# Two-level Strassen products in a gated FNet mix: the last couple of sequence product 3 at the second level, and four inner sums made by accumulating transfers

## The chip, the cores and the metric

The kernel runs on one core of one Trainium2 chip. The metric is the device time of one execution in microseconds; for the kernel before it is 1760.47 us, the median of three runs (1760.24 to 1760.79).

## The reference, cut to what matters

All matrices are float32: x is 2048 x 1024 (S x D), the sequence DFT 2048 x 2048, the hidden DFT 1024 x 1024, w1 1024 x 3584, w2 3584 x 1024.

```python
g = sigmoid((x * gate_w).sum(-1, keepdims=True))
a = einsum("bsd,ed->bse", x, dft_hid_re)
b = einsum("bsd,ed->bse", x, dft_hid_im)
y = einsum("ts,bse->bte", dft_seq_re, a) - einsum("ts,bse->bte", dft_seq_im, b)
h = einsum("bsd,df->bsf", x, w1) + b1
h = where(h > 0, h, 0) ** 2
out = g * y + (1 - g) * (einsum("bsf,fd->bsd", h, w2) + b2)
```

## The kernel before, in words

**Runs and products.** There are five large matrix products, which the code calls runs: x (both hidden DFTs), a and b (the two column parts of w1), c (the sequence DFT, its real and imaginary half stacked to 8 k-steps of 256 rows) and o (w2, 7 k-steps of 256). Each run is done with Strassen's scheme in Winograd's form: both matrices are cut in 2 x 2 quadrants, and seven products of sums of quadrants take the place of eight. `FACTORS` (line 40) names the left and the right factor of the seven: product 1 takes the quadrants (0, 0) and (0, 0), product 2 (0, 1) and (1, 0), product 3 the left sum S4 and the right quadrant (1, 1), product 4 (1, 1) and T4, and 5 to 7 take S1 and T1, S2 and T2, S3 and T3. "c3" is product 3 of the run c. `ORDER` (line 27) is the order in which TensorE takes the products of all runs: the three runs x, a, b first, then c1, c2, c5, c6, c3, c7, o1, c4, o2, o5, o6, o3, o7, o4.

**The second level.** Inside a product the scheme is used once more. In c and o (function `tall`, line 738) two k-steps that follow each other form a couple; the couple's 2 x 2 blocks are multiplied with seven inner products in place of eight. `TWICE_C` and `TWICE_O` (lines 37 and 38) say how many couples of a product are taken so; the k-steps that are left over are multiplied plainly, as `rest` (lines 767 and 869). Of the eight k-steps of a product of c, four couples use all and leave no `rest`; three couples leave two k-steps.

**Steps and matmuls.** A step is one left operand of 256 columns against one right operand of 512. A number in float32 is split in two float32r parts, `hi` (a conversion on ScalarE, line 238) and `lo` (the remainder, on VectorE, lines 244 and 246), and a step multiplies hi by hi, hi by lo and lo by hi. With two row blocks of 128 and two halves of the contraction that is 2 x 2 x 3 = 12 matmuls of 128x128 against 128x512 in c and o. A couple has seven steps; two plain k-steps have eight, for two left row halves against two right columns each.

**Sums.** The left sums of a couple are made in `Lefts` (line 463): S1 and S2 side by side in one tile, the difference S3 beside the first block, and S4, each by VectorE on 128x512, with 3.5 operands of 512 columns in all. The right ones are made in `Inner` (line 404) by `add` (line 214), one VectorE instruction of 128x1024 each. For couples whose first right block is kept in "turned" form, made ahead of time and stored, `TURN_R_SUMS` gives T2 as block (0, 1) plus block (0, 0), T1 as block (1, 1) less T2, and T4 as block (1, 0) less T2. A plain k-step whose block is stored turned needs one difference to turn it back (`plain_right`, line 829).

The sums of the outer level are made in `Side` (line 370). `BY_DMA` (line 63) names those that a transfer makes, for how many eighths of the positions: `accumulate` (line 203) loads one addend through SyncE's queue and lets GpSimd issue a transfer that adds the other from memory into the same tile. `THROUGH_C` (line 124) says for how many k-steps the outer sum T2 of c, made for c6 and used again in c4, is stored to memory and loaded again; for the others its tile is held from c6 to c4.

**Results of a product.** A product of c has four quarter results of two row blocks. Where another product's result has to be added (`old`), it is added by VectorE as soon as the first inner products are there, and the sum is reloaded into PSUM by ScalarE (`Group`, with `onto`) before the last inner products are summed onto it. With `late` (line 809, from `LATE`) the old result itself is reloaded, and what the product made is added at the end. A fourth group, for the plain k-steps alone, exists only where there is a `rest`.

**Order of the work.** TensorE's order is fixed. All other operations are entered in a list with the time at which they are needed: a step's operands by the step's place in TensorE's order, less a lead from `LEADS`, and everything before them backwards from there. A pass that is run when the program is built then gives each engine its own fixed order: at each moment it takes the first operation of the engine whose inputs are there, not more than `AHEAD` us before its due start, if one of the 55 tiles of 128x1024 float32 is free (`try_engine`, line 1566). `HALF` limits how many operands may have their `hi` without their `lo`. On the chip each engine then runs its order with semaphore waits only. `EARLY`, `TURNED_L` and `GATE` give dates to sums and differences that are made long before they are used. Loads go through SyncE's queue, stores and accumulating transfers through GpSimd's.

The matmuls are issued in line 1699; the sums of `add` are line 217, the left sums lines 481, 483, 488, 499 and 517, the additions from PSUM lines 356 and 358, the additions of two tiles line 366, the reloads of PSUM line 292.

Of the kernel before, what the change touches and what calls it, by code (L numbers as in the profile page):

```python
# [33 lines left out]
TWICE_X = (1, 2, 4, 5, 6, 7, 3)  # L34
TWICE_HA = (2, 3, 4, 5, 6, 7, 1)
TWICE_HB = (2, 4, 5, 6, 7, 1, 3)
TWICE_C = {1: 4, 2: 4, 3: 3, 4: 4, 6: 4, 5: 4, 7: 3}
TWICE_O = {1: 3, 2: 3, 3: 3, 4: 3, 6: 3, 7: 3, 5: 3}

FACTORS = {1: ((0, 0), (0, 0)), 2: ((0, 1), (1, 0)), 3: ("S4", (1, 1)), 4: ((1, 1), "T4"), 5: ("S1", "T1"),  # L40
# [19 lines left out]
MIX_R = {"T1": ((0, 0), (0, 1), ADD), "T2": ((1, 1), "T1", SUB), "T3": ((0, 1), (1, 1), SUB),  # L60
         "T4": ("T2", (1, 0), ADD)}
LESS_X, LESS_H, LESS_C, LESS_O = (3, 4), (3, 4, 5), (2, 6), (3, 4, 5)
BY_DMA = {'x_l': {'S1': 4, 'S2': 8, 'S3': 8, 'S4': 7}, 'x_r': {'T1': 5, 'T4': 8}, 'h_l': {'S4': 8, 'S3': 1}, 'c_l':
          {'S1': 7, 'S2': 7, 'S3': 8, 'S4': 8}, 'c_r': {'T1': 8, 'T2': 8, 'T3': 8, 'T4': 8}, 'o_l': {'S3': 8, 'S4':
          8}, 'o_r': {'T1': 8, 'T2': 8, 'T3': 8, 'T4': 8}}

AHEAD = {'SP': 13.4041, 'POOL': 13.1802, 'ACT': 13.8196, 'DVE': 10.3962}
FILL = {'DMA': 1.0243, 'ACT': 0.9397, 'DVE': 0.9869}
TAKE = 5.665
MARGIN = 0.79  # L70
NEAR = 0.0
URGENT = 1.997
KEEP = 5
EAGER = True
WARM = 38
LATE = {'c': (3,), 'o': (4, 5, 6, 7)}
DISTANT = (28.14, 4)
NARROW = (11.07, 3, 0.0)
LEADS = {208: 3.25, 209: 2.48, 210: 0.01, 212: 0.01, 213: -2.5, 186: 3.07, 216: 5.65, 199: 9.25, 200: 6.08, 201:
# [16 lines left out]
HURRY = 2.54  # L96
HALF = (2, 2.79)
BACKLOG = {"SP": 3.0, "POOL": 3.0}
PRELOAD = 30.0
EARLY_Q = (0, 1, 2, 3, 4, 5, 6, 7)  # L100
# [2 lines left out]
SUMMED = "xab"  # L103
ADD_S = ""
ADD_U = "bx"
EARLY = {'a_l': (('S2', 'S1'), (), 103.56, 2.103), 'b_l': (('S2',), (), 78.82, 4.245), 'x_r': (('T1',), (), 53.81,
         5.58)}
MERGE = 'sma'
STORES = "POOL"
# [2 lines left out]
REST = 0.886  # L112
GUARD = (0.874, 5.533)
SOON = {'POOL': 12.044, 'ACT': 5.5589, 'DVE': 6.9021}
SLACK = {'SP': 2.4281, 'POOL': 1.2495, 'ACT': 0.592, 'DVE': 0.4891}
LEAD = {'SP': 2.8064, 'POOL': 1.2123, 'ACT': 1.9836, 'DVE': 2.6943}
GATE = (268.4, 9.31)
WINDOW = 100
C_FORMS = ()
O_FORMS = ()  # L120
THROUGH_X = ("S1", "S2")
THROUGH_H = ("S2",)
THROUGH_W = ()
THROUGH_C = {'T2': 5}
THROUGH_O = {'T2': 8, 'S1': 2, 'S2': 2}
TURN_R = {'c': (0, 1, 2, 3), 'o': (0, 1, 2)}
TURN_L = {'c': (0, 1, 2), 'o': (0, 1)}
THIRD = {"c": (), "o": ()}
BACKWARD = {'c': (1, 4), 'o': (6,)}
TURNED_L = (((0, 0), (0, 1), (1, 0), (1, 1)), 100, 40)  # L130
TURNED_EARLY = (((0, 1), (1, 1), (0, 0), (1, 0)), 133, 30)
TURN_R_SUMS = {"T2": ((0, 1), (0, 0), ADD), "T1": ((1, 1), "T2", SUB), "T4": ((1, 0), "T2", SUB)}


@with_exitstack
def gated_mix_kernel(ctx: ExitStack, tc: tile.TileContext, x4, xn, w4, ct, w1a, w1b, w2, b1, b2, gw, out):
# [66 lines left out]
    def accumulate(v, src):  # L203
        w = Val("sum", v.width)
        Op("POOL", 0.6, 2 * P * 4 * v.width * 2, [v, src], w,
           lambda: nc.gpsimd.dma_start(w.ap(), src.at, accum_op=ADD), over=[v], must=True)
        return w
# [530 lines left out]
    def tall(name, left, right, ksteps, order, second, less, final, from_ps, by_row=None, turn=None, plain=None, turn_l=None,  # L738
# [5 lines left out]
        def product(p, old, quad):  # L744
# [45 lines left out]
            def inner(q):  # L790
                if q not in TURN_R[name]:
                    return Inner(lambda j, c: block(q, j, c), INNER_R)
                made = {}
                if turn and r in turn:
                    made[0, 1] = turn[r](q, block(q, 0, 1), block(q, 1, 1))
                inner_ = Inner(lambda j, c: block(q, j, c), TURN_R_SUMS)
                inner_.made.update(made)
                return inner_
# [1034 lines left out]
```

## Time and profile before

| | |
|---|---|
| median of three runs | 1760.47 us |
| the profiled execution, its own time | 1760.47 us |
| its span, first to last instruction | 1758.6 us |
| TensorE matmul, busy | 1752.1 us, 7748 instructions |
| VectorE, busy | 1700.1 us, 1659 instructions |
| ScalarE, busy | 1085.2 us, 1209 instructions |
| GpSimd, busy | 324.8 us, 468 instructions |
| mean busy share of the DMA engines, by slices of the span | 0.5 to 0.9 and more |
| bytes moved | 531.03 MB, 302 GB/s |
| granted clock of TensorE | 0.999 of full speed |

The 7748 matmuls are 38 small ones that warm the engine up and 7710 of the products. The profile's window view cuts the span into stretches and gives the busy time of each engine in each; its stretches are put at the borders of the products, which follow from the count of matmuls. A busy time there is the union of the engine's instructions, so that the overlap of one instruction's end with the next one's start is not counted twice. In the waits, a wait of a DMA queue (SPq) is one of the queue's own instructions, before it issues a transfer. In the names, PE is TensorE, DVE VectorE, ACT ScalarE, POOL GpSimd and SP SyncE. A tile that an operation overwrites in place keeps its old name, so an accumulating transfer can stand as `raw<-in_ct` on POOL's queue.

### The profile page before, as it was taken

To read this page: it belongs to the slowest core of one execution; us is meant where nothing else is said; L and a number is where in the kernel's file an instruction comes from. 1 tells how busy PE (TensorE), PEld (TensorE's weight loads), DVE (VectorE), ACT (ScalarE), POOL (GpSimd) and SP (SyncE) were. 2 spreads that over 40 slices of the span, in tenths; PEclk is the share of its full clock that TensorE was granted. 3 is DMA by queue.
4 is the path that set the end of the run, shared out by engine and by line. 5 is a ranking of instruction groups with operands and counts; after the bars stand their busy time and mean duration, and the time that the engine had idled before them with its cause. 6 is when DMAs were issued, how large, how long until landed. Compare 5 with 4: busy or idle time off the path is not lost.

```text
span 1758.6 us, 21932 instructions
## 1 busy us (share of the span) xinstructions
PE 1752.1 (100%) x7748; PEld 1451.3 (83%) x7748; DVE 1700.1 (97%) x1659; ACT 1085.2 (62%) x1209; POOL 324.8 (18%) x468
## 2 busy tenths in 40 slices
PE   9999999999999999999999999999999999999998
PEld 8888888888888888888888888888888888888887
DVE  8989999999999999899999999999999999999997
ACT  7445743334659674886747667475675676657754
POOL 0112212012211222101223121202101123212120
PEclk9999999999999999999999999999999999999999
DMA  9989999999999999889999999999859999999994
GB/s 354 413 324 349 358 375 380 397 342 362 328 346 352 337 290 329 305 304 272 281 259 191 278 294 296 271 337 274 233 164 335 330 262 290 308 282 296 277 224 79
DMA packets 156079, 531.03 MB, mean 302 GB/s; under 512 B 17057, under 2 KB 30721, under 8 KB 155969
## 3 DMA queue, kind: packets, MB, share of 16 engines
q0 software_dynamic: 65440, 233.88, 50.6%
q1 hardware_dynamic: 89824, 294.57, 44.9%
q8 instruction: 61, 1.00, 0.2%
q10 hardware_dynamic: 704, 1.18, 0.2%
q14 instruction: 50, 0.40, 0.1%
HBM read 401.10 MB, written 128.47 MB: 301 GB/s over the span
## 4 chain that ended last, share of the span: by engine, by line
PE 99%; DMA 0%; DVE 0%; ACT 0%; issue 0%
PE ps L1699 99%; DMA raw<-in_x 0%; ACT hi L1738 0%; DVE o L1212 0%; DVE o L1214 0%
## 5 line engine op out<-in xcount | busy, mean ns | idle before, releaser
L1699 PE MATMUL ps<-hi 128*128 128x512 f32 x2350 | 912.9, 389 | 0.6 <-ACT hi L1738 0.6
L1699 PE MATMUL ps<-lo,hi 128*128 128x512 f32 x2350 | 912.7, 389 | 0.0
L1699 PE MATMUL ps<-hi,lo 128*128 128x512 f32 x2350 | 912.7, 389 | 0.0
L1699 PEld LDWEIGHTS ps<-hi 128*128 128x128 f32 x2350 | 441.1, 188 | 92.2 <-ACT hi L1738 0.7
L1699 PEld LDWEIGHTS ps<-hi,lo 128*128 128x128 f32 x2350 | 441.2, 188 | 91.7
L1699 PEld LDWEIGHTS ps<-lo,hi 128*128 128x128 f32 x2350 | 441.2, 188 | 91.5
L238 ACT ACTIVATE hi<-raw 128x1024 fp32r<-128x1024 f32 (+1 forms) x402 | 406.3, 1040 | 169.5 <-PE ps L1699 91.4
L246 DVE TENSOR_TENSOR lo<-raw,hi 128x1024 fp32r<-128x1024 f32 (+1 forms) x348 | 411.4, 1204 | 2.8 <-DMA raw<-ab 1.3
L238 ACT ACTIVATE hi<-sum 128x1024 fp32r<-128x1024 f32 (+1 forms) x290 | 295.4, 1035 | 169.2 <-DVE sum L217 78.8
L246 DVE TENSOR_TENSOR lo<-sum,hi 128x1024 fp32r<-128x1024 f32 (+1 forms) x236 | 280.1, 1201 | 4.0 <-PE ps L1699 1.9
L345 ACT ACTIVATE acc<-ps 128x1024 f32<-128x1024 f32 (+1 forms) x153 | 150.9, 991 | 158.7 <-PE ps L1699 142.3
L358 DVE TENSOR_TENSOR acc<-acc,ps 128x1024 f32<-128x1024 f32 (+1 forms) x142 | 159.0, 1127 | 19.9 <-PE ps L1699 19.3
L1699 PE MATMUL ps<-hi,both 128*128 128x512 f32 x440 | 144.1, 389 | 0.0
L217 DVE TENSOR_TENSOR raw<-raw 128x1024 f32<-128x1024 f32 (+1 forms) x114 | 130.4, 1160 | 0.0
L292 ACT ACTIVATE ps<-acc 128x1024 f32<-128x1024 f32 (+1 forms) x79 | 77.2, 981 | 83.8 <-DVE acc L358 49.7
L1699 PEld LDWEIGHTS ps<-hi,both 128*128 128x128 f32 x440 | 82.6, 188 | 17.1
L217 DVE TENSOR_TENSOR sum<-raw,sum 128x1024 f32<-128x1024 f32 (+1 forms) x81 | 96.3, 1189 | 0.4 <-PE ps L1699 0.3
L1699 PE MATMUL ps<-lo,both 128*128 128x512 f32 x220 | 85.6, 389 | 0.0
L366 DVE TENSOR_TENSOR acc<-acc 128x1024 f32<-128x1024 f32 x69 | 83.0, 1215 | 1.2 <-ACT acc L345 1.2
L358 DVE TENSOR_TENSOR back<-back,ps 128x1024 f32<-128x1024 f32 x64 | 71.2, 1122 | 1.9 <-PE ps L1699 1.2
L217 DVE TENSOR_TENSOR sum<-raw 128x1024 f32<-128x1024 f32 (+1 forms) x57 | 68.1, 1197 | 2.0 <-DMA ab<-back 1.9
L244 DVE SCALAR_TENSOR_TENSOR lo<-raw,hi 128x1024 fp32r<-128x1024 f32 (+1 forms) x54 | 63.3, 1176 | 4.7 <-ACT hi L238 4.0
(96 smaller groups left out, 1051.3 us busy)
## 6 DMA issues: line engine op xcount, KB each, us to landing
raw<-in_ct SPq DMA_DIRECT2D x104, 512.0 KB, 7.4
raw<-h SPq DMA_DIRECT2D x79, 512.0 KB, 9.6
raw<-in_w SPq DMA_DIRECT2D x75, 512.0 KB, 9.1
back<-v SPq DMA_DIRECT2D x54, 512.0 KB, 8.1
raw<-ab SPq DMA_DIRECT2D x42, 512.0 KB, 7.1
raw<-h POOLq DMA_DIRECT2D x42, 512.0 KB, 11.6
raw<-in_ct POOLq DMA_DIRECT2D x41, 512.0 KB, 11.7
sum<-t SPq DMA_DIRECT2D x36, 512.0 KB, 8.5
```

Source lines behind the costliest of these rows:

```text
L217: Op("DVE", c, l, [a, b], w, lambda: nc.vector.tensor_tensor(w.ap(), a.ap(), b.ap(), op=op), over=[a, b])
L238: nc.scalar.activation(self.hi()[:, k, :], src(v)[:, k, :], AF.Copy, scale=-1.0 if less else 1.0)
L244: nc.vector.scalar_tensor_tensor(a, b, -1.0, c, op0=ALU.mult, op1=SUB)
L246: nc.vector.tensor_tensor(a, b, c, op=SUB)
L292: lambda rp=rp, k=k, e=e, v=v: nc.scalar.activation(self.ps[rp][:, :k, :], v.tile[:, e:e + k, :], AF.Copy),
L345: group.take(seg, rp, Op("ACT", c, l, [], w, lambda: nc.scalar.activation(view(w.tile, rows, rp), view(group.ps[rp], rows, rp), AF.Copy, s ...
L358: nc.vector.tensor_tensor(a, b, d, op=ADD)
L366: Op("DVE", c, l, [a, b], w, lambda: nc.vector.tensor_tensor(view(w.tile, rows, rp), view(a.tile, rows, rp), view(b.tile, rows, rp), op=op ...
L1699: nc.tensor.matmul(group.ps[r // group.per][:, r % group.per, :], a()[:, kk, r * P:(r + 1) * P], b()[:, kk, :], start=first and kk + n == ...
```

## The change

1. `TWICE_C[3]` goes from 3 to 4: the k-steps 6 and 7 of c3 become a fourth couple.
2. A new table `T2_DMA` and two lines in `inner`: for product 1 of c and product 2 of o, the inner right sum T2 of the couples 0 and 1 is made by an accumulating transfer. It loads block (0, 1) into a tile of its own and adds block (0, 0) from memory. The blocks themselves are still loaded as operands.
3. `THROUGH_C` goes from 5 to 8: the outer sum T2 of c is stored and loaded again for all eight k-steps.
4. `BY_DMA`: of the sums T4 of the x run three of four positions are made by transfers, where it was all four; of the sums S3 of w1's left side one position of four, where it was none (1 and 3 eighths of four positions make none and one), in each of a and b.
5. `LATE` takes in the products 1 and 2 of c beside 3. Product 1 has no old result, so only c2 is different.
6. Numbers of the pass that orders the work: leads, limits and dates.

```diff
-TWICE_C = {1: 4, 2: 4, 3: 3, 4: 4, 6: 4, 5: 4, 7: 3}
+TWICE_C = {1: 4, 2: 4, 3: 4, 4: 4, 6: 4, 5: 4, 7: 3}
...
-BY_DMA = {'x_l': {'S1': 4, 'S2': 8, 'S3': 8, 'S4': 7}, 'x_r': {'T1': 5, 'T4': 8}, 'h_l': {'S4': 8, 'S3': 1}, 'c_l':
+BY_DMA = {'x_l': {'S1': 4, 'S2': 8, 'S3': 8, 'S4': 7}, 'x_r': {'T1': 5, 'T4': 7}, 'h_l': {'S4': 8, 'S3': 3}, 'c_l':
...
-AHEAD = {'SP': 13.4041, 'POOL': 13.1802, 'ACT': 13.8196, 'DVE': 10.3962}
+AHEAD = {'SP': 12.9725, 'POOL': 13.1802, 'ACT': 13.8196, 'DVE': 10.3962}
...
-URGENT = 1.997
+URGENT = 1.945
...
-LATE = {'c': (3,), 'o': (4, 5, 6, 7)}
+LATE = {'c': (1, 2, 3), 'o': (4, 5, 6, 7)}
...
-LEADS = {208: 3.25, 209: 2.48, 210: 0.01, 212: 0.01, 213: -2.5, 186: 3.07, 216: 5.65, 199: 9.25, 200: 6.08, 201:
+LEADS = {208: 3.25, 209: 2.48, 210: 0.01, 212: -2.5, 213: -2.5, 186: 3.07, 216: 5.65, 199: 9.25, 200: 6.08, 201:
...
-HALF = (2, 2.79)
+HALF = (3, 2.85)
...
-EARLY = {'a_l': (('S2', 'S1'), (), 103.56, 2.103), 'b_l': (('S2',), (), 78.82, 4.245), 'x_r': (('T1',), (), 53.81,
+EARLY = {'a_l': (('S2', 'S1'), (), 103.56, 2.103), 'b_l': (('S2',), (), 93.23, 3.09), 'x_r': (('T1',), (), 53.81,
...
-SLACK = {'SP': 2.4281, 'POOL': 1.2495, 'ACT': 0.592, 'DVE': 0.4891}
-LEAD = {'SP': 2.8064, 'POOL': 1.2123, 'ACT': 1.9836, 'DVE': 2.6943}
-GATE = (268.4, 9.31)
+SLACK = {'SP': 2.4281, 'POOL': 1.2741, 'ACT': 0.592, 'DVE': 0.4891}
+LEAD = {'SP': 2.8064, 'POOL': 0.954, 'ACT': 1.9836, 'DVE': 2.6943}
+GATE = (244.0, 12.76)
...
-THROUGH_C = {'T2': 5}
+THROUGH_C = {'T2': 8}
...
-TURNED_L = (((0, 0), (0, 1), (1, 0), (1, 1)), 100, 40)
+TURNED_L = (((0, 0), (0, 1), (1, 0), (1, 1)), 64.3, 44.13)
...
+T2_DMA = {'c': {1: 2}, 'o': {2: 2}}
...
                 made = {}
+                if q < T2_DMA[name].get(p, 0) and isinstance(r, tuple):
+                    made["T2"] = accumulate(right[2 * q, 1].of(r), right[2 * q, 0].get(*r))
                 if turn and r in turn:
```

Of `LEADS`, a table from a step's number to us, about half of the entries differ and some hundred are new; one line of it stands here.

## Rows read from the trace of the kernel before

**Rows 1.** Waits of TensorE: line, waited for: us in total, times, longest.

```profile
PE warm L1748 <- DVE ones L1745: 1.1, 1, 1.1
PE ps L1699 <- ACT hi L1738: 0.6, 1, 0.6
```

**Rows 2.** The chain that ended last, in order of time: start us, us, what.

```profile
0.74 3.96 DMA raw<-in_x
...
5.71 1748.03 PE ps L1699 x7710
```

**Rows 3.** Windows: length, busy us (instructions) PE, PEld, DVE, ACT, POOL; clock, DMA share, GB/s.

```profile
738.90:815.10 76.20, 76.20 (x338) 63.12 (x337) 76.20 (x78) 57.36 (x64) 5.14 (x10) 1.00 0.85 301
815.10:891.30 76.20, 76.20 (x337) 62.95 (x336) 74.43 (x72) 51.61 (x54) 16.48 (x20) 1.00 0.97 265
...
967.50:1043.60 76.10, 76.10 (x337) 63.06 (x336) 75.22 (x76) 49.23 (x53) 13.08 (x18) 1.00 0.98 292
1043.60:1122.50 78.90, 78.90 (x349) 65.35 (x349) 74.23 (x72) 48.39 (x51) 16.47 (x21) 1.00 1.03 287
1122.50:1201.40 78.90, 78.90 (x349) 65.34 (x348) 78.39 (x77) 45.92 (x48) 9.80 (x14) 1.00 0.93 294
1201.40:1269.50 68.10, 68.10 (x302) 56.41 (x301) 68.10 (x68) 46.39 (x49) 13.29 (x16) 1.00 0.99 279
1269.50:1345.60 76.10, 76.10 (x338) 63.02 (x337) 73.61 (x72) 50.24 (x53) 3.36 (x5) 1.00 0.65 234
1345.60:1413.70 68.10, 68.10 (x302) 56.43 (x301) 68.10 (x65) 43.42 (x48) 12.04 (x15) 1.00 0.99 298
...
5.70:738.90 733.20, 733.19 (x3235) 607.28 (x3236) 701.66 (x685) 418.69 (x494) 138.64 (x229) 1.00 0.99 351
738.90:1685.70 946.80, 946.80 (x4178) 784.08 (x4177) 936.33 (x915) 623.37 (x665) 176.58 (x226) 1.00 0.97 278
```

**Rows 4.** Waits of VectorE from 738.9 to 1685.7 us: total, times, longest.

```profile
DVE acc L358 <- PE ps L1699: 2.8, 1, 2.8
DVE lo L246 <- PE ps L1699: 2.6, 5, 1.3
DVE lo L246 <- DMA raw<-ab: 1.3, 1, 1.3
```

**Rows 5.** Waits of SyncE's DMA queue from 738.9 to 1753 us.

```profile
SPq L200 <- PE ps L1699: 428.3, 138, 13.6
```

**Rows 6.** Timeline of VectorE at the end of c3: start us, us, instruction.

```profile
1092.22 4.62 DVE L246 TENSOR_TENSOR lo<-raw,hi 128x1024 fp32r<-128x1024 f32 x4
1096.76 1.21 DVE L217 TENSOR_TENSOR sum<-raw 128x1024 f32<-128x1024 f32 x1
1097.90 0.68 DVE L481 TENSOR_TENSOR sum<-raw 128x512 f32<-128x512 f32 x1
1098.50 3.48 DVE L246 TENSOR_TENSOR lo<-raw,hi 128x1024 fp32r<-128x1024 f32 x3
...
1105.38 4.61 DVE L246 TENSOR_TENSOR lo<-raw,hi 128x1024 fp32r<-128x1024 f32 x4
...
1114.57 1.22 DVE L358 TENSOR_TENSOR acc<-acc,ps 128x1024 f32<-128x1024 f32 x1 [2.83 <-PE ps L1699]
```

**Rows 7.** DMA issues: queue, count, KB each, median us to landing.

```profile
raw<-in_ct SPq DMA_DIRECT2D x104, 512.0 KB, 7.4
raw<-h SPq DMA_DIRECT2D x79, 512.0 KB, 9.6
...
raw<-h POOLq DMA_DIRECT2D x42, 512.0 KB, 11.6
raw<-in_ct POOLq DMA_DIRECT2D x41, 512.0 KB, 11.7
sum<-t SPq DMA_DIRECT2D x36, 512.0 KB, 8.5
...
raw<-turned SPq DMA_DIRECT2D x20, 512.0 KB, 6.3
```

38 rows, old and new, of the table LEADS are left out of this document.

## The prediction

> **What bounds the kernel now.** I read the waits of TensorE first: after its 38 warm-up matmuls it waits once, 0.6 us, for the first operand [rows 1]. Then the chain that ended last: 3.96 us of the first load, its conversion, and from 5.71 us on 7710 matmuls in 1748.03 us without a hole [rows 2]. That is 1748.03 / 7710 = 0.22672 us a matmul. So the time is the number of matmuls times 0.22672, with 5.71 us ahead of it and 4.9 us behind it in the span of 1758.6. The profiled execution took 1760.47 us, which is also the median of the three runs; the 1.9 us beside the span stay.
>
> The matmuls cut the span into products: the x, a and b products take 3234 matmuls, so c1 begins at 5.71 + 3234 x 0.22672 = 738.9; a product of c with four couples takes 28 x 12 = 336, one with three 348, one of o 300. In the windows by product, TensorE is busy for the whole of each, at a granted clock of 1.00, the level of 2.4 GHz [rows 3]. The second column to read is VectorE's: 76.20 of 76.20 in c1, 68.10 of 68.10 in o1 and o2. From c1 to the end of o7 it is busy 936.33 of 946.80 us, so it idles 10.47 us; in c3 it idles 4.67, in c4 2.49, in c2 1.77 [rows 3]. Its waits in that stretch are for a matmul to end or a transfer to land, few and short [rows 4]. Loads are not late either: SyncE's queue itself waited 428.3 us in 138 waits for TensorE to give a tile free [rows 5]. TensorE is the wall, VectorE stands just behind it, and tiles limit how far ahead the rest can work.
>
> **The change, part by part.** *The fourth couple of c3.* Two k-steps taken plainly cost 2 x 4 steps = 96 matmuls; as a couple they cost 7 steps = 84. Twelve fewer, 7698 in all: 12 x 0.22672 = 2.72 us off TensorE. No other part touches the count of matmuls.
>
> VectorE pays for it. Its pace is read from starts, since one instruction's end overlaps the next: four of 128x1024 start at 1092.22 and the next at 1096.76, so 4.54 / 4 = 1.135 us each; one of 128x512 at 1097.90 is followed at 1098.50, so 0.60 [rows 6]. Plainly the two k-steps need 2 left and 4 right low parts and one right difference: 7 wide instructions. As a couple they need 7 right and 3 left wide low parts, the right sums T2, T1, T4 (13 wide), and on the left one narrow low part and four narrow sums (5 narrow). 13 x 1.135 + 5 x 0.60 - 7 x 1.135 = +9.81 us. Quarter results cost the same: one addition from PSUM becomes one from tiles. ScalarE gets 4.5 more conversions and loses one reload of PSUM, some 4 us; it is busy 48.39 of 78.90 in c3 [rows 3], so nothing. The number of loads doesn't change: five right tiles either way.
>
> *T2 by transfer.* Four wide sums leave VectorE, two in c1 and two in o2: 4 x 1.135 = 4.54 us less. Each becomes one more load on SyncE's queue and an accumulating transfer on GpSimd's. Accumulates of this kind, with tiles as destination, land in 11.7 us (from the matrix, c1) or 11.6 us (from h, o2), after a load of 6.3 or 9.6 us [rows 7]. Through VectorE the chain is a load of 7.4 and 1.135 us. Started at the same moment, the new chain for c1 is 6.3 + 11.7 - 7.4 - 1.1 = 9.5 us later. I take nothing for it on TensorE: the schedule issues loads ahead of need, and 83 accumulates of these two kinds are already there [rows 7] without one wait of TensorE [rows 1]. The cover is the tile held about 10 us longer; if it is gone, T1, which subtracts T2, is late, then its two parts, then a step. Bounds: 0, and 9.5 us for each of four couples, 38 us. In GpSimd's queue the accumulate waits for its load; behind it stand the stores of c1's quarters, read much later, and o2's other accumulates, operands of o5. GpSimd is busy 5.14 us of c1 and 12.04 of o2 [rows 3], so little queues there.
>
> First the row: a plain load of the matrix by SyncE lands in 7.4 us, the accumulate by GpSimd in 11.7 [rows 7]. The Trainium skill says in "DMA: Bandwidth & Descriptors" (SWDGE vs HWDGE vs iDMA) that only GpSimd can issue accumulating transfers, and in "SBUF — State Buffer" (Who interferes with whom) that a VectorE instruction with two SBUF inputs contends with GpSimd's reads, and that a transfer held up by VectorE is one GpSimd makes. By that rule moving a sum off a full VectorE puts it on the one queue that a full VectorE can hold up, and the sum would be that of the late accumulates below; the longer landing agrees in sign, but the row can't say how much of it is the addition itself.
>
> *T2 of the outer sums through memory for k-steps 5 to 7.* Six stores more in c6 and six loads more in c4; six tiles are no longer held across c3, c7 and o1. c4's transfers are busy 0.65 of the time, c6's 0.98 [rows 3]. At nothing: o1's 68 us cover the loads for c4's first couple. Above: one load late, 8.5 us [rows 7]. Below: the free tiles let VectorE work further ahead, which can remove idle time there but no matmul.
>
> *The rest.* Of the left sums S3 one position of four goes to transfers in a and in b, and one T4 of the x stage comes back to VectorE: about one addition fewer before c1, where VectorE idles 31 us of 733 [rows 3]. c2's old quarters join at the end instead of midway: ten VectorE instructions and three reloads both ways. The new leads, dates and limits only reorder. All nothing, between -0.3 and +0.3 us, since TensorE's start hangs on the first load alone [rows 2] and nothing but a wait can add.
>
> **The sum** against the profiled execution: 1760.47 - 2.72 = 1757.75, if TensorE still never waits. Whether it does is VectorE's balance. From c1 to o7: 936.33 + 9.81 - 4.54 = 941.60 us of work in 946.80 - 2.72 = 944.08, so 2.48 us of idle time may stay of 10.47. In c3 alone, 74.23 + 9.81 = 84.04 us of work meet 78.90 - 2.72 = 76.18: 7.86 too much. Working ahead in c1's freed 2.27 us leaves 5.6 us by which VectorE comes closer to TensorE than before. How far ahead was it there? At 1105.38 it already made the first four low parts of c7, whose matmuls begin at 1122.5, 17 us later, and then sat idle 2.83 us for a matmul to end [rows 6]. Five and a half of these 17 us can go. After that c7's and c4's idle time (0.51 + 2.49) and o2's 2.27 give 5.3 back. So the likeliest is no wait: 1757.8.
>
> **Rivals.** *Some of the lead is missing where it is needed.* VectorE comes 5.6 us closer at c7's start, a few operands come late, and TensorE waits 0.6 to 6 us in all: 1758.4 to 1764. For it: VectorE is at 100% in c1, o1 and o2. Against: its lead of 17 us. Chance 0.20, more of it at the low end.
>
> *VectorE becomes the bound (the other side).* Its idle time is not lead to spend but made of waits that come again: for matmuls to end (2.8 and 2.6 us) and for transfers (1.3 us) [rows 4]. If all 10.47 us stay, TensorE must give 10.47 - 2.48 = 8.0 us, and the time is 1765.8. It decides slower once more than 6.24 + 2.48 = 8.7 us of the 10.47 stay, since 2.72 + 3.52 us must be lost (0.2% is 3.52 us, about what a measurement of this kernel can tell from no change). Against: in c3 half of the idle time is 2.83 us at its end with c7's work already made. Chance 0.08.
>
> *Late accumulates.* One couple late by the whole 9.5 us gives 1767.3, all four 1795.8. Against: the 83 that are on time. Chance 0.03.
>
> *It doesn't do it.* If the fourth couple were not taken, the count stayed 7710 and the time 1760.5; the code leaves no such way. Chance 0.01.
>
> *Faster by over 0.2%.* 3.52 us need another 0.8 us from the start or the end, which hang on the first load and the last two additions; 0.03.
>
> **How the numbers follow.** The forecast, no wait beyond 0.6 us, has 0.65. Within 0.2%: 0.65 + 0.20 + 0.01 = 0.86; slower 0.08 + 0.03 = 0.11; faster 0.03. The range begins at 1757.2 (a start half a microsecond sooner) and reaches to 1761.5, which takes in about three quarters of the waiting case, 0.15: 0.80 in all.
>
> **What would show it.** Right: 7698 matmuls after the warm-up in about 1745.3 us, no wait of TensorE longer than 0.6 us, c3's window at 76.2 us with VectorE full and its 2.83 us wait gone; VectorE's busy time about 4.4 us up (9.81 - 4.54 - 0.9); 42 loads of stored sums into a sum's tile where there were 36 [rows 7]; 20 transfers of 512 KB more in all. Wrong: TensorE waiting for a low part or its sum near 1120 to 1200, or for T1 in the second half of c1 or the first of o2 with an accumulate as its cause; or VectorE idle by 10 us again while TensorE waits.

## The result, and the profile after

The changed kernel takes **1763.66 us** (median of 15 runs, 1762.94 to 1765.52) against 1760.50 for the kernel before beside it (15 runs): ratio 1.0016, 95% interval 1.0009 to 1.0023. It is slower by 3.2 us, which is within 0.2%. The profiled execution took 1763.37 us with a span of 1761.5. The forecast was 1757.8, the range ended at 1761.5.

The page of the kernel after: busy time of each engine with its share of the span and its instructions, then the two lines of the chain that ended last.

```profile
PE 1751.3 (99%) x7736; PEld 1448.0 (82%) x7736; DVE 1704.6 (97%) x1665; ACT 1089.3 (62%) x1213; POOL 332.6 (19%) x479
...
PE 95%; DVE 3%; DMA 1%; issue 1%; POOL 0%; ACT 0%; DVEq 0%
PE ps L1710 95%; DVE lo L255 1%; DMA t<-raw 1%; DVE lo L253 0%; DVE sum L226 0%; DVE back L375 0%; DMA raw<-in_x 0%; DVE acc L375 0%; DVE sum L526 0%; DVE o L1223 0%; DVE o L1225 0%; DVE sum L492 0%; DVE raw L226 0%; DVE both L253 0%; ACT h
```

TensorE issued 7736 matmuls where it had 7748: the twelve are gone. VectorE is 4.5 us busier than before. But the chain, which was TensorE alone from 5.71 us on [rows 2], now leaves it for VectorE, 3% of the span. The waits of TensorE (line, waited for: us in total, times, longest; the lines of the code behind the edit in `inner` stand 11 lower than before, so 1710 is 1699 of [rows 1]; those between the tables and that edit stand 9 lower, so 255 is 246 and 226 is 217):

```profile
PE ps L1710 <- DVE lo L255: 3.7, 4, 1.5
...
PE ps L1710 <- ACT hi L1749: 0.5, 1, 0.5
```

Four waits for low parts are new. The view counts only a gap behind a matmul's modelled end; counted by starts, that is as the distance from one matmul's start to the next, it is more. The first matmul starts at 5.45 us and the last at 1756.28, and 7697 steps of 0.22672 us are 1745.06, so 1756.28 - 5.45 - 1745.06 = **5.8 us** is waiting. The account closes: -2.72 for the matmuls, -0.26 for the earlier start, +5.8 for the waits are +2.8 of the 2.9 us between the two profiled executions. So the saving came in full, and twice as much was lost to waits. Where, the windows by product show (length, busy us of PE, PEld, DVE, ACT, POOL with their instructions; clock, DMA share, GB/s), in the order c1, c2, c5, c6, c3, c7, o1, as [rows 3] has them but for c5:

```profile
738.60:814.80 76.20, 76.20 (x338) 62.89 (x337) 76.20 (x77) 58.27 (x66) 7.99 (x13) 1.00 0.91 319
814.80:891.00 76.20, 76.20 (x338) 63.10 (x337) 71.74 (x69) 48.77 (x51) 13.71 (x17) 1.00 0.92 263
891.00:968.60 77.60, 76.44 (x338) 62.98 (x337) 74.95 (x75) 51.57 (x56) 26.12 (x33) 1.00 1.04 230
968.60:1046.50 77.90, 76.42 (x337) 62.73 (x336) 77.75 (x80) 53.02 (x56) 16.60 (x24) 1.00 1.01 311
1046.50:1124.40 77.90, 76.81 (x338) 63.07 (x337) 77.90 (x76) 47.92 (x50) 14.44 (x18) 1.00 0.98 279
1124.40:1203.40 79.00, 78.97 (x349) 65.06 (x348) 79.00 (x78) 46.66 (x49) 9.96 (x13) 1.00 1.04 337
1203.40:1271.80 68.40, 68.36 (x301) 56.13 (x301) 68.40 (x67) 45.67 (x48) 12.87 (x16) 1.00 0.99 284
```

c5, c6 and c3 should last 336 x 0.22672 = 76.2 us and last 77.6, 77.9 and 77.9. In c6, c3, c7 and o1 VectorE is busy 303.05 of 303.20 us: it has nothing left. In c6 alone it runs 80 instructions where it ran 76 [rows 3], in c3 76 for 72. Yet just ahead of that stretch it sits idle: 4.46 us in c2 and 2.65 in c5, together 7.1, where it was 1.77 [rows 3] and 0.11, by the window of c5 before:

```profile
891.30:967.50 76.20, 76.20 (x338) 63.09 (x337) 76.09 (x77) 49.53 (x53) 24.63 (x31) 1.00 1.01 220
```

What it waited for there (from 738.6 to 968.6 us):

```profile
DVE lo L255 <- PE ps L1710: 3.5, 5, 1.3
DVE sum L526 <- PE ps L1710: 2.0, 1, 2.0
DVE lo L253 <- ACT hi L247: 0.7, 1, 0.7
DVE sum L436 <- PE ps L1710: 0.4, 1, 0.4
...
```

Nearly 6 of the 7 us are waits for a matmul to end. A low part and a sum read nothing that TensorE makes, so what a matmul's end gives them must be the tile to write to, which TensorE has then read for the last time; this is inferred from who ended the wait. The first wait of TensorE, at 914.45 us, is such a case itself. The chain around it, start us, us, what:

```profile
899.91 13.16 PE ps L1710 x58
...
913.17 1.24 DVE lo L255
...
914.45 5.74 PE ps L1710 x24
```

A matmul ends, that lets one low part start, and the next matmul waits 1.4 us for this part. The second and third wait, 1.6 us at 1014.30 and 1.5 from 1050.44 on by starts, are of the other kind. The second, in the timeline of TensorE and of VectorE (start us, us, instruction, idle time before it and who ended that); from 984 to 1053 us VectorE has no idle time:

```profile
1012.43 0.39 PE L1710 MATMUL ps<-hi 128*128 128x512 f32 x1
1014.30 0.50 PE L1710 MATMUL ps<-lo,hi 128*128 128x512 f32 x1 [1.48 <-DVE lo L255]
```

```profile
1012.41 0.69 DVE L526 TENSOR_TENSOR sum<-raw,sum 128x512 f32<-128x512 f32 x1
1013.02 2.36 DVE L255 TENSOR_TENSOR lo<-raw,hi 128x1024 fp32r<-128x1024 f32 x2
```

The third:

```profile
1049.60 0.39 PE L1710 MATMUL ps<-hi 128*128 128x512 f32 x1
1050.44 0.50 PE L1710 MATMUL ps<-lo,hi 128*128 128x512 f32 x1 [0.45 <-DVE lo L255]
1051.58 0.50 PE L1710 MATMUL ps<-hi,lo 128*128 128x512 f32 x1 [0.63 <-DVE lo L255]
```

```profile
1040.60 4.64 DVE L255 TENSOR_TENSOR lo<-raw,hi 128x1024 fp32r<-128x1024 f32 x4
1045.14 1.24 DVE L226 TENSOR_TENSOR raw<-raw,sum 128x1024 f32<-128x1024 f32 x1
1046.28 2.38 DVE L255 TENSOR_TENSOR lo<-sum,hi 128x1024 fp32r<-128x1024 f32 x2
1048.55 0.71 DVE L492 TENSOR_TENSOR sum<-sum,raw 128x512 f32<-128x512 f32 x1
1049.15 3.51 DVE L255 TENSOR_TENSOR lo<-raw,hi 128x1024 fp32r<-128x1024 f32 x3
```

Two low parts in a row come late, by 0.61 and 0.91 us, while VectorE goes from one instruction to the next without a gap. Here its order holds more work than there is time. The store in the page's chain (`DMA t<-raw`, 17.65 us up to 1040.23) kept nothing waiting: the low part behind it starts at 1040.60, 1.14 us after VectorE's instruction ahead of it, which is VectorE's own pace.

### The profile page after: what moved, and what is told of

Its sections match the earlier page's. It is cut to its first block, busy times and chain, and to the rows that moved or that the text cites. A ratio compares the mean times of both kernels' runs of the same rounds, so it can differ in the third digit from the quotient of the medians.

```text
span 1761.5 us, 21886 instructions
## 1 busy us (share of the span) xinstructions
PE 1751.3 (99%) x7736; PEld 1448.0 (82%) x7736; DVE 1704.6 (97%) x1665; ACT 1089.3 (62%) x1213; POOL 332.6 (19%) x479
## 2 busy tenths in 40 slices
DMA packets 158958, 541.52 MB, mean 307 GB/s; under 512 B 17376, under 2 KB 31040, under 8 KB 158848
## 4 chain that ended last, share of the span: by engine, by line
PE 95%; DVE 3%; DMA 1%; issue 1%; POOL 0%; ACT 0%; DVEq 0%
PE ps L1710 95%; DVE lo L255 1%; DMA t<-raw 1%; DVE lo L253 0%; DVE sum L226 0%; DVE back L375 0%; DMA raw<-in_x 0%; DVE acc L375 0%; DVE sum L526 0%; DVE o L1223 0%; DVE o L1225 0%; DVE sum L492 0%; DVE raw L226 0%; DVE both L253 0%; ACT hi L1749 0%
## 5 line engine op out<-in xcount | busy, mean ns | idle before, releaser
L255 DVE TENSOR_TENSOR lo<-raw,hi 128x1024 fp32r<-128x1024 f32 (+1 forms) x349 | 421.1, 1235 | 3.7 <-PE ps L1710 1.8
L247 ACT ACTIVATE hi<-sum 128x1024 fp32r<-128x1024 f32 (+1 forms) x294 | 299.8, 1037 | 164.1 <-DVE sum L226 92.5
L255 DVE TENSOR_TENSOR lo<-sum,hi 128x1024 fp32r<-128x1024 f32 (+1 forms) x239 | 288.5, 1225 | 4.7 <-PE ps L1710 2.4
L367 DVE TENSOR_TENSOR acc<-acc,ps 128x1024 f32<-128x1024 f32 (+1 forms) x144 | 162.7, 1137 | 14.8 <-PE ps L1710 12.1
L226 DVE TENSOR_TENSOR raw<-raw 128x1024 f32<-128x1024 f32 (+1 forms) x116 | 134.5, 1178 | 0.0
L226 DVE TENSOR_TENSOR sum<-raw,sum 128x1024 f32<-128x1024 f32 (+1 forms) x77 | 92.7, 1208 | 0.7 <-PE ps L1710 0.5
L215 POOL DMA_DIRECT2D raw<-h x44 | 41.1, 1069 | 135.2 <-DMA raw<-h 56.2
## 6 DMA issues: line engine op xcount, KB each, us to landing
raw<-h POOLq DMA_DIRECT2D x44, 512.0 KB, 11.7
t<-raw POOLq DMA_DIRECT2D x40, 512.0 KB, 14.4
```

Of the source, the lines that this page charges most:

```text
L226: Op("DVE", c, l, [a, b], w, lambda: nc.vector.tensor_tensor(w.ap(), a.ap(), b.ap(), op=op), over=[a, b])
L247: nc.scalar.activation(self.hi()[:, k, :], src(v)[:, k, :], AF.Copy, scale=-1.0 if less else 1.0)
L255: nc.vector.tensor_tensor(a, b, c, op=SUB)
L367: nc.vector.tensor_tensor(a, b, d, op=ADD)
```

## The experiments

Three theories stand. **Work** (A): with the couple, VectorE has more to do between c5 and o1 than that stretch holds, and TensorE waits for what is left over. **Order and tiles** (B): the work would fit, but low parts stand too far back in VectorE's fixed order or find no tile. **The side effects**: the accumulating transfers come late (C), or c2's late join moves additions into the full stretch (D). A further question came up with the first answers (E in the expectations): is the time that VectorE has ahead of the full stretch of any use in it? There A1 is theory A (the amount of work decides), and A2 says that its place and order do.

In the numbers below, VectorE's idle time in a product is the product's length less VectorE's busy time in it, with the borders put at the product's first matmuls; TensorE's wait is that length less the number of matmuls times 0.22672 us. For the change that gives 1.4 us of waits in c5, 2.0 in c6, 1.6 in c3, 0.3 in c7 and 0.4 in o1.

### The order kept, less work in c5, c6 and c3 (e_cut)

```diff
         Op("DVE", c, l, [a, b], w, lambda: nc.vector.tensor_tensor(
...
+        cut = 203 <= len(steps) < 287
...
+            n = 16 if cut and (w.tile is a.tile or w.tile is b.tile) else 512
+            nc.vector.tensor_tensor(view(w.tile, rows, rp)[:, :, :n], view(a.tile, rows, rp)[:, :, :n],
+                                    view(b.tile, rows, rp)[:, :, :n], op=op)
```

> The changed kernel in the same order on every engine; 14 of VectorE's additions of two tiles in c5, c6 and c3 work on 16 of 512 columns (those sums are left out). That takes 14 x some 1.0 us of VectorE's time out of this stretch and nothing else. Theory A (VectorE's work: the couple's 9.8 us is fetched forward into c5 and c6, which were full): the four waits of TensorE of 1.4 to 1.8 us at 914, 1014, 1050 and those of 0.3 after them vanish but for at most 1 us in all, and the time is 1757.8 to 1759. Rival B (tiles: an operand's low part waits until TensorE gives its tile free): the waits stay, 1762 or more. Rival C (the new stores and accumulates land late): the waits stay, 1762 or more.

Measured: 1759.58 us against 1760.68, ratio 0.9994 (0.9985 to 1.0003), 4 us less than the change. Where VectorE then has no wait, as behind ten of the 14, a cut addition is followed 0.10 us later by the next instruction where it was 1.135, so some 14.5 us of VectorE's time are free. The first of the 14 ran early, in c2 at 862 us, and 13 in c5, c6 and c3. The waits of TensorE:

```profile
PE ps L1716 <- DVE lo L255: 1.3, 2, 1.2
...
PE ps L1716 <- ACT hi L1755: 0.2, 1, 0.2
```

By starts 1.5 us remain in c5 and 0.5 in c6, and none in c3, so the time lies between the two forecasts. With VectorE's work cut, and every engine's order the same, the waits at 1050 and behind it go, and most of the one at 1014: they want VectorE's time, and not a tile. Whether that is too much work or work in the wrong place this run does not tell, since four of the cut additions stand at 1004 to 1008 and at 1015.9 us, around the late low part of 1014, and what is cut ahead of a low part also brings it forward. The wait at 914 stays, and with it B for that one place. Of the 14.5 us, 4 came back as time of the program and 9 as idle time of VectorE from c2 to c3.

### The couple alone, in the kernel before (e_couple)

```diff
-TWICE_C = {1: 4, 2: 4, 3: 3, 4: 4, 6: 4, 5: 4, 7: 3}
+TWICE_C = {1: 4, 2: 4, 3: 4, 4: 4, 6: 4, 5: 4, 7: 3}
```

The leads of all steps behind c3's last are moved by one, since c3 has one step fewer.

> The kernel before with the fourth couple of c3 alone (leads of the steps from c7 on moved by one step, since c3 has one step fewer). Theory A: VectorE has 9.8 us more and nothing is taken from it, so TensorE waits in c5 to c7 more than in the changed kernel, over 6 us in all: 1764 or more. Rival C (the waits come from the new transfers): no new transfers, so no waits, 1757.8.

Measured: 1776.51 us, ratio 1.0091 (1.0076 to 1.0106). C, by which there should have been no wait without the new transfers, is refuted. The waits come late, 1.9 us in c6, 4.7 in c3, 10.7 in c7 and 2.0 in o1, and VectorE idles 7.95 us in c7 beside them. Two of TensorE's waits, 2.4 and 1.7 us by the view, are for ScalarE. So the couple without the rest of the change is far worse than with it: the pass puts its work in a bad order here, which a count of work alone does not tell. Part of the loss is the clock's; the last section shows it.

### The transfers without the couple (e_t2_th)

```diff
-THROUGH_C = {'T2': 5}
+THROUGH_C = {'T2': 8}
...
+T2_DMA = {'c': {1: 2}, 'o': {2: 2}}
...
+                if q < T2_DMA[name].get(p, 0) and isinstance(r, tuple):
+                    made["T2"] = accumulate(right[2 * q, 1].of(r), right[2 * q, 0].get(*r))
```

> The kernel before with T2 by transfer (four sums) and the outer T2 of all eight k-steps through memory, without the couple; leads and limits as before. Theory A: VectorE has 4.5 us less work, TensorE has all its matmuls and no new wait: 1760.5, within 0.7 us. Rival C: the accumulates and stores alone make TensorE wait 3 us or more: 1763.5 or more.

Measured: 1760.95 us, ratio 1.0001 (0.9991 to 1.0010). Waits of TensorE:

```profile
PE ps L1702 <- DVE lo L247: 0.2, 1, 0.2
```

Four accumulates in place of four sums, six stores and six loads through memory, and 0.2 us of waiting by the view, 0.5 in c5 by starts, that was not there before. The transfers cost nothing that can be measured (C falls), and the 4.54 us they take off VectorE bring nothing as long as VectorE keeps up.

### c2's quarters joined midway again (e_notlate)

```diff
-LATE = {'c': (1, 2, 3), 'o': (4, 5, 6, 7)}
+LATE = {'c': (3,), 'o': (4, 5, 6, 7)}
```

> The changed kernel with c2's old quarters added midway, as before (LATE of c only 3). Rival D (the late join pushes four additions, 4.5 us, from c2 into the full c5 and leaves VectorE idle in c2): the waits shrink by 3 us or more, 1760.5 or less. Theory A: the amount of VectorE's work is the same, the waits stay within 2 us or grow: 1762 to 1766.

Measured: 1768.80 us, ratio 1.0049 (1.0032 to 1.0066): 5 us worse than the change, with waits of 3.2 us in c5, 2.6 in c6 and 4.4 in c3. That the late join is the cause, as D had it, is refuted in this form; A's 1766 is passed as well. The pass makes the whole order anew, though, so the run does not say how much is the join and how much the order.

### The same couple, order fitted anew (e_refit_b, e_refit_a)

Two kernels for which leads and limits of the pass were fitted again; the leads, replaced as a whole, are not shown here or below. The first (e_refit_b) has the couple and `THROUGH_C` 8, but neither `T2_DMA` nor the late join; the second (e_refit_a) is the change itself.

```diff
...
-TAKE = 5.665
-MARGIN = 0.79
+TAKE = 5.503
+MARGIN = 0.701
...
-URGENT = 1.997
+URGENT = 2.051
...
-HURRY = 2.54
-HALF = (2, 2.79)
+HURRY = 1.894
+HALF = (2, 2.89)
...
-REST = 0.886
+REST = 0.46
...
-THROUGH_C = {'T2': 5}
+THROUGH_C = {'T2': 8}
```

> The kernel before with the couple and the outer T2 through memory, no inner T2 by transfer and no late join; the leads and four limits of the ordering pass are fitted anew to the 28 steps of c3. VectorE has all of the couple's 9.8 us and nothing is taken off it, so its work from c1 to o7 is 4.5 us more than in the changed kernel. Theory A1 (the amount decides: 946.2 us of work in 944.1): TensorE must wait 2 us or more and the time is 1760 or more. Theory A2 (place and order decide: idle time that VectorE has in c2, c5 and c4 is spent ahead): the waits are under 2 us and the time is 1757.8 to 1759.5, under both kernels.

Measured for e_refit_b: 1761.32 us, ratio 1.0003 (0.9995 to 1.0012). From c1 to o1 VectorE idles 1.6 us in all and TensorE waits 3.3 us, 2.2 of them in c6. A1 said 2 us or more, and A2, under 2 us, fails for this order. This is the cleanest view of the work itself: VectorE has hardly any idle time left to recover, and the couple still gives back all that it saves.

```diff
-TAKE = 5.665
-MARGIN = 0.79
+TAKE = 5.658
+MARGIN = 0.651
...
-URGENT = 1.945
+URGENT = 2.338
...
-HURRY = 2.54
-HALF = (3, 2.85)
+HURRY = 2.066
+HALF = (3, 2.41)
...
-REST = 0.886
+REST = 0.772
```

> The changed kernel, all its parts, with leads and limits fitted anew. Theory A2: the same work on every engine in another order, so the waits of 5.7 us fall below 2.5 us and the time is 1757.8 to 1760.2; VectorE's idle time in c2 and c5, 7.1 us in the changed kernel, falls. Theory A1: the amount of work hasn't changed, waits of 4 us or more stay: 1762 or more.

Measured for e_refit_a: 1762.84 us, ratio 1.0015 (1.0006 to 1.0023). VectorE still idles 4.89 us in c2, and the largest wait, 3.7 us in all, moves to c6. Another order of the same work lands within 1 us of the change, as A1 had it.

### The change without the accumulates (e_not2)

```diff
-T2_DMA = {'c': {1: 2}, 'o': {2: 2}}
+T2_DMA = {'c': {}, 'o': {}}
```

> The changed kernel with the four inner sums T2 made by VectorE again, as before. Theory A: VectorE gets 4.5 us of work back, half of it in c1 just ahead of the full stretch: more waits, 1765 to 1771. Rival C (the accumulates cause the waits): fewer waits, 1761 or less.

Measured: 1769.18 us, ratio 1.0050 (1.0036 to 1.0063), with 2.5 us of waits ahead of c1, 2.5 in c5, 1.8 in c6, 2.6 in c3. VectorE has the four sums back, 4.54 us, and the program is 5.5 us longer. If late accumulates were the cause, it should have become shorter. How much of the 5.5 us is the sums the run does not say: the order is made anew here too, and the waits ahead of c1, of which the largest is 1.3 us at 470 us, lie ahead of every sum that the edit touches.

### The late join without the couple (e_t2_th_late)

The kernel e_t2_th with one line more:

```diff
-LATE = {'c': (3,), 'o': (4, 5, 6, 7)}
+LATE = {'c': (1, 2, 3), 'o': (4, 5, 6, 7)}
```

> The kernel before with the inner T2 by transfer, the outer T2 through memory and c2's late join, without the couple. Beside the run without the late join (1760.95) it prices that join alone. Rival D: four additions moved into the full c5 cost TensorE a wait near 915 to 925 of 1.5 us or more: 1762 to 1763.5. Theory A: without the couple VectorE has room, no wait over 0.6 us: 1760.5 to 1761.2.

Measured: 1762.55 us, ratio 1.0011 (1.0002 to 1.0021), 1.6 us more than e_t2_th. TensorE's timeline in c5:

```profile
918.16 0.39 PE L1702 MATMUL ps<-hi 128*128 128x512 f32 x1
919.84 0.50 PE L1702 MATMUL ps<-lo,hi 128*128 128x512 f32 x1 [1.30 <-DVE lo L247]
```

1.46 us by starts. VectorE runs back to back ahead of it, from 904 to 919.8 us. What the join moved stands in the groups of VectorE in c5, multiplications by the gate, in e_t2_th and then here:

```profile
L1124 DVE TENSOR_TENSOR y<-ps,g 128x1024 f32<-128x1024 f32 x1 | 1.2, 1209 | 0.0
```

```profile
L1124 DVE TENSOR_TENSOR acc<-acc,g 128x1024 f32<-128x1024 f32 x3 | 3.7, 1219 | 0.0
```

Two such multiplications and an addition (3 x 1.135 = 3.4 us) left c2, where VectorE idles 3.3 us, for c5, where it idles 1.6. The wait stands where D had put it, so D holds for this pair of orders: 1.6 us with the join, without the couple. It is no price of the join in every order: e_refit_a above and e_t2_c3, e_refit_c and e_refit_d below have the join and no wait in c5.

### T2 made by transfer in c3 instead of c1 (e_t2_c3)

```diff
-T2_DMA = {'c': {1: 2}, 'o': {2: 2}}
+T2_DMA = {'c': {3: 2}, 'o': {2: 2}}
```

> The changed kernel with one table changed: the two inner sums T2 that transfers make in c1 are made by VectorE there and by transfers in c3 instead; o2 as in the changed kernel, all leads and limits too. Theory E (VectorE's time is needed where the couple is; what is freed in c1 can't be carried to c3, since VectorE then runs out of tiles and idles in c2): the waits of 5.7 us fall below 3 us, 1758 to 1761. Theory A1 (the amount alone decides; it is the same): the waits stay, 1762.5 to 1765. Rival C (accumulates land late, c3's DMA share was 0.98): the waits grow, 1765 or more.

Measured: 1762.36 us, ratio 1.0011 (1.0002 to 1.0019). From c5 to o1 TensorE waits 3.2 us instead of 5.8, but 1.0 us of new waits come in c1, from which the relief was taken. With 4.1 us in all it lies between the forecasts, below 3 us for E and unchanged for A1. It fits E that the same two sums are worth more where the work was added; but the order is made anew, so 1.3 us alone would not show it.

### The same, order fitted anew, twice (e_refit_c, e_refit_d)

```diff
-MARGIN = 0.79
+MARGIN = 0.725
...
-URGENT = 1.945
+URGENT = 2.091
...
-HURRY = 2.54
-HALF = (3, 2.85)
+HURRY = 3.429
+HALF = (3, 2.58)
...
-REST = 0.886
+REST = 0.871
```

> The kernel with T2 by transfer in c3 and o2, with leads and limits fitted anew. Theory E: VectorE has 2.3 us less to do in the full stretch, which leaves room to reorder: waits of 0 to 1.5 us, 1757.8 to 1759.3, under both kernels. Theory A1: 1761 or more, as the other kernels fitted anew.

Measured for e_refit_c: 1760.49 us, ratio 1.0001 (0.9992 to 1.0009). It is the best version of the couple, 3.2 us better than the change and no better than the kernel before; its waits come to 2.6 us, about the saving of 2.7, and 1.5 of them are in c1. Neither forecast holds: E's 1759.3 is passed, A1's 1761 not reached. By the view, which leaves out gaps that a matmul's modelled end covers:

```profile
PE ps L1686 <- DVE lo L231: 0.8, 2, 0.6
PE ps L1686 <- ACT acc L330: 0.3, 1, 0.3
```

The second fit starts from the same kernel.

```diff
-MARGIN = 0.79
+MARGIN = 0.768
...
-URGENT = 1.945
+URGENT = 1.987
...
-HURRY = 2.54
-HALF = (3, 2.85)
+HURRY = 2.128
+HALF = (3, 3.19)
...
-REST = 0.886
+REST = 0.708
```

> A second fit of the same kernel, found from another start: it tells how much of the gain hangs on one order. Theory E: 1757.8 to 1760. Theory A1: 1761 or more.

Measured for e_refit_d: 1764.05 us, ratio 1.0021 (1.0011 to 1.0030), with 3.6 us of waits ahead of c1 (0.9 us each at 652 and 729 us, 1.0 at its end), ahead of the products whose T2 the edit moves. E missed, and the pair is a measure: two orders of one and the same work stand 3.6 us apart, so a difference of that size between two whole programs says little about the work.

From c1 on, the orders differ less. There the waits by starts are 5.7 us in the change and 5.0 in e_refit_a, the same work; 3.2 in e_refit_b; 4.1 in e_t2_c3, 2.7 in e_refit_c and 2.5 in e_refit_d, which have the same work once more. No order tried got below 2.5 us, about what the couple saves.

### The order kept, less work ahead of the full stretch (e_cut_c2)

```diff
+        cut = 147 <= len(steps) < 203
...
+            n = 16 if cut and (w.tile is a.tile or w.tile is b.tile) else 512
...
+                    e = 16 if quad == (0, 0) and v and w.tile is v.tile else 512
+                    nc.vector.tensor_tensor(w.tile[:, :, :e], source()[:, :, :e], gates[:, :, :e], op=ALU.mult)
```

> The changed kernel in the same order on every engine; eight of VectorE's instructions of c1 and c2 (four additions of two tiles, the four multiplications of c2's results by the gate) work on 16 of 512 columns; those values are left out. That takes some 8 us of VectorE's time out ahead of 901 us, as the other cut took 14 us out, most of it behind. Theory E (time freed ahead of the full stretch can't be carried into it): VectorE idles longer for tiles in c2 and c5, and TensorE's waits at 914, 1014 and 1050 stay, 4 us or more of 5.7; 1762 or more. Theory A1 (the amount alone decides): 8 us of lead cover all waits, 1759 or less.

Measured: 1763.65 us, ratio 1.0018 (1.0009 to 1.0028), the same as the change. Waits of TensorE, and the windows of c1, c2 and c5:

```profile
PE ps L1717 <- DVE lo L255: 3.7, 4, 1.5
...
```

```profile
738.60:814.80 76.20, 76.20 (x338) 63.12 (x337) 75.35 (x78) 58.72 (x66) 7.32 (x12) 1.00 0.93 321
814.80:891.00 76.20, 76.20 (x338) 63.12 (x337) 68.64 (x69) 49.53 (x52) 14.38 (x18) 1.00 0.92 259
891.00:968.60 77.60, 76.44 (x338) 62.99 (x337) 71.63 (x75) 50.52 (x55) 25.51 (x32) 1.00 1.04 230
```

The four waits are those of the change, 3.7 us in 4, to the tenth. Some 8 us were freed (8 instructions x 1.03), and 7.3 of them are found again as idle time: 0.85 + 7.56 + 5.97 = 14.4 us in c1, c2 and c5, where it was 7.1. What it waits for there:

```profile
DVE lo L255 <- PE ps L1717: 6.5, 8, 1.7
DVE sum L532 <- PE ps L1717: 3.1, 2, 2.0
DVE sum L501 <- PE ps L1717: 1.7, 1, 1.7
...
```

Beside e_cut this settles the further question for this order. Time taken off VectorE inside the full stretch took 4.0 us of the 5.8 us of waits away; taken off just ahead of it, it turns into waiting for a matmul to end, and nothing of it arrives.

## Why the prediction was wrong

**The saving was right.** 7698 matmuls at 0.22672 us; the twelve are worth 2.72 us, and the account of the two executions closes with it.

**The counts were right.** VectorE's busy time went from 1700.1 to 1704.6 us, 4.5 up where 4.4 was forecast; bytes from 531.03 to 541.52 MB, which is 20 transfers of 524,288 bytes; and the loads of stored sums are 42 where [rows 7] has 36. The issues after (queue, count, KB, median us to landing):

```profile
raw<-h POOLq DMA_DIRECT2D x44, 512.0 KB, 11.7
sum<-t SPq DMA_DIRECT2D x42, 512.0 KB, 10.1
...
raw<-in_ct POOLq DMA_DIRECT2D x38, 512.0 KB, 12.5
```

**T2 by transfer and through memory at nothing: right.** The accumulates land in 11.7 and 12.5 us, about as before [rows 7]; e_t2_th is at 1.0001, and e_not2 is worse without them. The bound of 38 us above was far from it. No run here shows an accumulate that TensorE waited for. The rival that the prediction drew from the Trainium skill, "SBUF — State Buffer" (Who interferes with whom), left out a sentence of that section: its probe saw `tensor_copy` stall transfers, but not `tensor_tensor`, which is 1480 of VectorE's 1665 instructions here.

**The balance failed.** The step was "936.33 + 9.81 - 4.54 = 941.60 us of work in 946.80 - 2.72 = 944.08, so 2.48 us of idle time may stay of 10.47". The terms are near (measured from c1 to o7: 940.4 us of work), the stretch is not. It counts idle time anywhere in 947 us as if it could be filled from anywhere else, and 2.27 us freed in c1 as if c3 could have them. e_cut_c2 shows that 8 us freed in c1 and c2 do nothing for c6 and c3. Over the stretch in which VectorE is full, c6, c3, c7 and o1, the same sum reads: idle before 0.88 + 4.67 + 0.51 + 0 = 6.06 us [rows 3], wanted 9.81 + 2.72 = 12.53, so 6.5 us are missing. TensorE's waits in these four products came to 4.3 us by starts and VectorE's idle time fell to 0.15. The rest is work that was done outside: VectorE is busy 303.05 us in them where it was 295.94 [rows 3], 7.1 more and not 9.8.

**"Five and a half of these 17 us can go" failed with it.** The 17 us of lead were read at c3's end, but the waits came at 1014 and 1050, before c3 was well begun. VectorE's order had taken up part of the couple's work there: four instructions more in c6, four more in c3. A lead read at the end of a stretch says nothing of the lead at its beginning. After 1051.58 us the chain has only two more short breaks, at 1138.95 and 1239.47, 0.3 us each by starts.

**c2's late join at nothing is open.** The instructions are as many, as counted, but three of them go from c2, with room, to c5, with little: 1.6 us without the couple (e_t2_th_late against e_t2_th). With the couple, taking the join back costs 5 us, and four orders that have it show no wait in c5, so no run gives the join's own price.

**The rivals.** "Some of the lead is missing where it is needed" gave 0.6 to 6 us of waits and 1758.4 to 1764; 5.8 us is its upper end, but in c5, c6 and c3's beginning, not at c7's start. The mechanism of the other side, that VectorE's idle time "is not lead to spend but made of waits that come again", describes the trace better: from c1 to o7 VectorE still idles 9.4 us (7.1 in c2 and c5, 1.0 in c4, 0.95 in o3, 0.4 elsewhere). Put into that rival's own sum, 9.4 - 2.48 = 6.9 us, 1764.7, it misses by 1.3 us, which is the work: 940.4 us where the sum had 941.6. Tiles stood in the rows before already: SyncE's queue waits 428 us for TensorE to give tiles free [rows 5], and the 2.6 us of VectorE's low parts in [rows 4] are waits for a matmul to end (the 2.8 us of the addition are for a result). The prediction concluded from them that tiles limit how far ahead the rest can work, and left that out of its balance.

**What stays open.** Why e_couple, e_notlate and e_not2 lose as much as they do: each makes the whole order anew, and e_refit_c and e_refit_d show that an order alone moves the time by 3.6 us. For the same reason it is not shown that no order of the couple's work is faster; nine kernels with the couple and all the work were run. That the tiles missing in c2 and c5 are held by work that was fetched ahead is inferred from who released the waits; a kernel with one more tile for low parts was not tried. None of the versions that do all the work beat the kernel before.

## What to carry to other kernels

When the first engine is full and the second nearly so, balance the second over the stretch that its buffers can bridge, not over the run: idle time on the far side of a buffer limit cannot be spent. Ask of a wait "for the first engine to end" on the second engine whether it is for a result or for a tile; a wait for a tile says that the lead is already at its limit. If an edit adds work to a full stretch, take the relief from the same stretch: two sums made by transfer in c3 in place of two in c1 took the waits behind c2 from 5.8 to 3.2 us, though 1.0 us came back in c1.

## What the runs showed of the hardware that was not expected

**The clock fell behind a wait in the middle of full work.** In e_couple, TensorE's starts and its granted clock around a wait in c3 (timeline, then windows with columns as above):

```profile
1061.24 0.39 PE L1683 MATMUL ps<-hi 128*128 128x512 f32 x1
1063.97 0.79 PE L1683 MATMUL ps<-lo,hi 128*128 128x512 f32 x1 [2.33 <-DVE lo L230]
1064.56 0.63 PE L1683 MATMUL ps<-hi,lo 128*128 128x512 f32 x1
...
1067.46 0.39 PE L1683 MATMUL ps<-hi 128*128 128x512 f32 x1
```

```profile
1064.40:1067.60 3.20, 3.20 (x9) 2.48 (x9) 2.92 (x3) 1.63 (x2) 0.00 (x0) 0.54 0.26 51
1067.60:1070.00 2.40, 2.40 (x13) 1.95 (x12) 1.65 (x2) 1.07 (x1) 0.00 (x0) 1.00 0.36 75
```

After 2.73 us from start to start, eight matmuls take 1067.46 - 1063.97 = 3.49 us where eight took 8 x 0.2267 = 1.81, at a granted 0.54, near the lower level of 1.2 GHz; then it is 1.00 again. So this wait of 2.5 us cost 4.2. The run has two more such stretches, behind 2.83 us at 1136.05 and 2.62 at 1156.33, with the granted clock at 0.50; in the three, matmuls at the lower pace cost 5.4 us of the 21 us that TensorE lost in this run. The length of the gap does not decide alone: in e_notlate 2.61 us at 916.10 are followed by matmuls 0.33 and 0.23 us apart at a granted 1.00. Behind the change's wait of 1.6 us at 1014.30 they are 0.34, 0.24 and 0.23 us apart, so nothing of the kind, and the windows after stay at 1.00.

**A recorded duration is not the pace.** In the changed kernel the recorded durations grow: an addition of 128x1024 is recorded with 1.22 us in c2 and about 1.28 in c7 of the same execution, while the starts stay 1.135 us apart:

```profile
1140.49 1.28 DVE L226 TENSOR_TENSOR sum<-raw 128x1024 f32<-128x1024 f32 x1
1141.62 1.28 DVE L255 TENSOR_TENSOR lo<-raw,hi 128x1024 fp32r<-128x1024 f32 x1
```

A sum made of the recorded durations would have given VectorE 7 to 13% more work than it has; the starts are what to count with. What makes them grow is open: in the kernel before they stay at 1.21 to 1.22 us, in o1 too, where VectorE is never idle either.
